# The second MLP's first layer as seven block products in place of eight

## Chip, core and metric

One core of a Trainium2 chip. The metric is the device time of one launch in microseconds, the median of the runs. TensorE (PE in the rows, PEld for its weight loads), VectorE (DVE), ScalarE (ACT) and GpSimd (POOL) each take their own instructions strictly in order; SyncE (SP) issues the DMAs, also in order.

## What is computed

Three stages, one behind the other, all in float32:

```python
attn = A @ Z @ C @ v                  # landmark attention, 4 batches of 576 tokens, 8 heads of 64
x = attn as [2304, 512]
h = x @ w_in                          # first MLP, 512 -> 2048 -> 512
x = (h - tanh(h)) @ w_out
h = x @ w_in2                         # second MLP, 512 -> 2048 -> 512
out = (h * tanh(softplus(h))) @ w_out2
```

The change is in the line `h = x @ w_in2`.

## The kernel before

Every matmul operand is split in a high part that TensorE takes exactly and a low part (`gg[:, 0]`, `gg[:, 1]` and the like); a product is three matmuls: high by high, high by low, low by high. ScalarE writes the high part by a copy, VectorE the low part by a subtraction.

**Stage one** runs in 128 slots (NS = 128; a batch has 32, each of 288 tokens by 128 hidden rows). A slot issues the first layer of its own block (`h1`), the second layer (`y1`) of the block three slots back (LAG = 3), and `vec`, the elementwise work. The attention of the next batch is strewn between. In the last 24 slots GpSimd is not used (`E()` gives VectorE). From slot 116 on the order of the engines is the order of the code; ahead of it a scheduler sets it. The results go to DRAM (`ys`).

**Stage two** has six chunks of 384 tokens by 16 blocks of 128 hidden rows: 96 slots. `h2` is 12 matmuls of 384 columns (4 pieces of the 512 inputs, 3 each), accumulated in one bank; ScalarE takes Mish of it twice (L600 writes the high part, L601 the whole), VectorE subtracts (L602); `o2`, three slots later, is 9 matmuls of 512 columns. The bank of `h2` is read by ScalarE alone, and the next slot but one writes it again.

Weights come as 64-bit numbers. `convert` brings them to float32 (a ScalarE cast at L133, a VectorE join at L137) and `split` to high and low (L102, L103). They are converted once, in the first two chunks of stage two, and all 32 blocks stay on the chip. Finished rows of the output leave from `raw` buffers, of which there are four, two tiles of 512 columns in each.

Of the kernel before, what the change touches and what calls it, by code (L numbers as in the profile page):

```python
# [29 lines left out]
def kernel(  # L30
# [150 lines left out]
    def convert(jobs, more=None):  # L181
        n = len(jobs)
        raws, st, parts2 = {}, {}, {}
        ahead = 4 if more else 3

        def fetch(i):
            if i < n:
                raws[i] = load_raw(jobs[i][0], more if more and i % 6 > 3 else None)
# [3 lines left out]
        for i in range(n + 2):  # L192
            if i < n:
                parts2[i] = f32_a(raws.pop(i), i)
            if i - 1 in parts2:
                where = jobs[i - 1][2]
                st[i - 1] = where() if where else st_p.tile([128, 512], F32, tag="y", name="y")
                yield from f32_b(*parts2.pop(i - 1), st[i - 1])
# [313 lines left out]
    W1o, W2i, W2o = {}, {}, {}  # L512
    yc, ops = {}, {}

    def tmp(s, tag, bufs=2):
        return tp[s >= NS].tile([128, width(s)], F32, tag=tag, name=tag, bufs=bufs)
# [15 lines left out]
    def cf(s):  # L532

        i = s - NS
        if i >= 32:
            return i // 16, i % 16
        n = PAIR - 16
        if i < 2 * n:
            return i % 2, i // 2
        return int(i >= PAIR), n + (i - 2 * n) % (16 - n)  # L540

    def h2(s):
        c, f = cf(s)
        y = yc[c]
        if s % 2 and s > NS + 32 + LAG:
# [391 lines left out]
```

## Time and profile before

| | |
|---|---|
| three runs | 840.97, 842.04 (median), 843.12 us |
| the profiled execution's own time | 840.79 us |
| its span | 839.0 us, granted clock 0.992 |
| TensorE busy | 811.1 us, 97% |
| VectorE, ScalarE, GpSimd busy | 473.0, 468.1, 179.4 us |

The span begins at the first and ends with the last record of the program; 1.8 us of the time lie around it. Times below are microseconds from the span's start. Stage two begins with the first `h2` at 428.7 us.

### The profile page before, as it was taken

The numbers are of one execution on the slowest core, as the hardware profiler recorded it, in microseconds if no ns is written. First come the engines' busy times: TensorE is split into PE (matmuls) and PEld (weight loads), VectorE is DVE, ScalarE is ACT, GpSimd is POOL, SyncE is SP. The second block draws the span as 40 slices with busy tenths as digits, with TensorE's granted clock in tenths as the row PEclk, the third lists the DMA queues.
The fourth block names the chain that finished last, engine by engine and source line by source line (L and its number), as shares of the span: only waits on it lengthen the run. The fifth ranks groups of instructions, "written<-read, shape, count | busy, mean of one in ns | idle before, by whom it ended". The sixth has DMA issues, their size and how long they took to land.

```text
span 839.0 us, 14649 instructions
## 1 busy us (share of the span) xinstructions
PE 811.1 (97%) x5528; PEld 696.4 (83%) x5528; DVE 473.0 (56%) x1093; ACT 468.1 (56%) x1163; POOL 179.4 (21%) x210
## 2 busy tenths in 40 slices
PE   4799999999999999999999999999999999999998
PEld 1446688789888988789999999999999999999996
DVE  7679999998799877899964744222112111111111
ACT  4576887888678976899765744233223223222221
POOL 0010006775588657840000000000000000000000
PEclk9699999999999999999999999999999999999999
DMA  9999341512135001451007741022002001000001
GB/s 323 321 336 356 111 138 52 170 67 90 54 104 182 2 30 38 136 165 47 3 1 270 253 132 45 1 66 76 0 1 69 8 1 57 9 1 24 15 1 38
DMA packets 34983, 79.57 MB, mean 95 GB/s; under 512 B 5472, under 2 KB 14176, under 8 KB 34912
## 3 DMA queue, kind: packets, MB, share of 16 engines
q1 hardware_dynamic: 33760, 74.45, 26.4%
q0 software_dynamic: 1152, 4.19, 1.2%
q8 instruction: 43, 0.70, 0.4%
q14 instruction: 28, 0.23, 0.1%
HBM read 65.00 MB, written 13.63 MB: 94 GB/s over the span
## 4 chain that ended last, share of the span: by engine, by line
PE 79%; DVE 9%; ACT 3%; POOL 2%; DMA 2%; issue 2%; DVEq 0%; SPq 0%; ACTq 0%; POOLq 0%
PE y L663 7%; PE y L659 7%; PE y L658 7%; PE h L553 5%; PE h L551 5%; PE h L552 5%; PE y L635 5%; PE y L639 5%; PE y L636 5%; PE h L525 4%; PE y L630 3%; PE m L217 3%; PE m L553 2%; PE m L551 2%; PE m L552 2%; DVE g L613 2%
## 5 line engine op out<-in xcount | busy, mean ns | idle before, releaser
L602 DVE TENSOR_TENSOR gg<-g,gg 128x384 fp32r<-128x384 f32 x96 | 53.6, 558 | 296.0 <-ACT g L601 296.0
L635 PE MATMUL y<-gg,w 128*128 128x288 f32 x448 | 133.7, 313 | 2.2 <-ACT raw L643 1.2
L636 PE MATMUL y<-gg,w 128*128 128x288 f32 x448 | 125.6, 295 | 0.0
L600 ACT ACTIVATE gg<-h 128x384 fp32r<-128x384 f32 x66 | 32.6, 494 | 142.3 <-PE h L553 142.3
L635 PEld LDWEIGHTS y<-gg,w 128*128 128x128 f32 x448 | 84.1, 188 | 22.2 <-issue 12.6
L659 PE MATMUL y<-w,gg 128*128 128x512 f32 x256 | 101.2, 395 | 0.0
L658 PE MATMUL y<-w,gg 128*128 128x512 f32 x256 | 100.8, 394 | 0.0
L639 PE MATMUL y<-gg,w 128*128 128x288 f32 x448 | 96.5, 297 | 0.4 <-POOL gg L103 0.2
L103 POOL TENSOR_TENSOR gg<-g,gg 128x288 fp32r<-128x288 f32 x80 | 69.5, 868 | 115.2 <-ACT gg L102 113.5
L663 PE MATMUL y<-w,gg 128*128 128x512 f32 x256 | 88.4, 396 | 0.0
L636 PEld LDWEIGHTS y<-gg,w 128*128 128x128 f32 x448 | 84.4, 188 | 1.1
L585 POOL TENSOR_SCALAR mk<-s 128x288 uint8<-128x288 f32 x80 | 77.4, 967 | 10.7 <-ACT s L579 4.4
L613 DVE COPY_PREDICATED g<-mk,th 128x288 f32<-128x288 uint8 x128 | 73.6, 575 | 4.2
L639 PEld LDWEIGHTS y<-gg,w 128*128 128x128 f32 x448 | 71.4, 188 | 1.9 <-POOL gg L103 1.7
L595 ACT ACTIVATE q<-q,bias_c 128x288 f32<-128x288 f32 x128 | 68.6, 536 | 2.3
L579 ACT ACTIVATE s<-h 128x288 f32<-128x288 f32 x128 | 52.0, 407 | 28.7 <-PE h L529 15.0
L591 DVE TENSOR_TENSOR g<-h,s 128x288 f32<-128x288 f32 x128 | 56.9, 445 | 18.4 <-ACT th L580 18.0
L553 PE MATMUL h<-yc,wj 128*128 128x384 f32 x192 | 64.6, 337 | 0.0
L600 ACT ACTIVATE gg<-m 128x384 fp32r<-128x384 f32 x30 | 14.8, 492 | 89.3 <-PE m L553 89.3
L552 PE MATMUL h<-yc,wj 128*128 128x384 f32 x192 | 64.4, 335 | 0.0
L551 PE MATMUL h<-yc,wj 128*128 128x384 f32 x192 | 64.4, 335 | 0.0
L609 DVE TENSOR_TENSOR g<-q,g 128x288 f32<-128x288 f32 x128 | 63.2, 494 | 1.4 <-ACT q L595 0.5
(162 smaller groups left out, 1833.4 us busy)
## 6 DMA issues: line engine op xcount, KB each, us to landing
w<-w1s SPq DMA_DIRECT2D x24, 512.0 KB, 4.7
raw<-in_w1i_dram SPq DMA_DIRECT2D x16, 511.8 KB, 6.4
raw<-in_w1o_dram SPq DMA_DIRECT2D x16, 511.8 KB, 6.8
raw<-in_w2i_dram SPq DMA_DIRECT2D x16, 511.8 KB, 4.7
raw<-in_w2o_dram SPq DMA_DIRECT2D x16, 511.8 KB, 4.2
ys<-raw SPq DMA_DIRECT2D x16, 288.0 KB, 2.3
out_dram<-raw SPq DMA_DIRECT2D x18, 256.0 KB, 2.3
v<-in_v_dram SPq DMA_DIRECT2D x8, 512.0 KB, 9.0
```

Of the source, the lines that this page charges most:

```text
L103: eng.tensor_tensor(out=L, in0=src, in1=f32(H), op=ALU.subtract)
L551: mm(p, w[:, 0, k, :], y[:, k, 0, :], start=(k == 0), stop=False)
L552: mm(p, w[:, 0, k, :], y[:, k, 1, :], start=False, stop=False)
L553: mm(p, w[:, 1, k, :], y[:, k, 0, :], start=False, stop=(k == 3))
L585: eng.tensor_scalar(out=mk, in0=e, scalar1=FT, scalar2=None, op0=ALU.is_ge)
L613: V.copy_predicated(out=g0, mask=mk0, data=t0)
L635: mm(yps[d], w[:, 0, c], gg[:, 0, :], start=(f == 0), stop=False)
L636: mm(yps[d], w[:, 1, c], gg[:, 0, :], start=False, stop=False)
L639: mm(yps[d], w[:, 0, c], gg[:, 1, :], start=False, stop=(f == NF - 1))
L658: mm(p, gg[:, 0, cs], w[:, 0, :], start=(f == 0), stop=False)
L659: mm(p, gg[:, 0, cs], w[:, 1, :], start=False, stop=False)
L663: mm(p, gg[:, 1, cs], w[:, 0, :], start=False, stop=(f == NF - 1))
```

## The change

Two chunks are one unit now (three units of 768 tokens), and two blocks of hidden rows one pair (eight). For a unit and a pair the product is a 2x2 by 2x2 product of blocks (inputs in two halves of 256, tokens in two of 384, hidden rows in two of 128). It is done with seven products of blocks in place of eight: four sums of blocks of x, four of the weights, seven of the results. So there are 24 **groups** (`group(k)`: unit k // 8, pair k % 8), each with seven **steps** p = 0 to 6. A step issues one product of 6 matmuls of 384 columns, then two units of the second layer of the group before (one in steps 5 and 6; 12 in all, 3 matmuls of 512 columns each), then `combine`.

- **Results.** `combine` adds a product from PSUM to a running sum in SBUF on VectorE (seven additions of 384, and one ScalarE copy at step 0). Mish reads the sums from SBUF, and the second Mish writes over its own input. The products have two banks (`ps_h`); the addition frees the bank for the next product but one.
- **Weights.** `w2_cycles` replaces `convert` for them. A cycle has seven parts, one per step; group k runs cycle k + 1 (cycle 0 lies in seven of the last 14 slots of stage one), and two last pieces of a group's own weights, the high and low part of `W2c[k][1]` slots 0 and 1, come in step 6 of the group before and step 0 of its own. Only the current weights of the first layer stay on the chip; `keep` writes them to DRAM (1.75 MB per pair), and groups 8 to 23 load them again (`w2c_load`, one group ahead).
- **Inputs.** `y_prep` makes the seven sums and parts of x for a unit: in nine slots from slot 102 on for the first unit (four sums of 768 columns on GpSimd), and next to groups 7 and 15 for the other two (two on GpSimd, two on VectorE). Its four loads go through the four `raw` buffers that the weights use.
- **Output.** The rows leave from the pool `st`, which has two buffers of 512 columns.

```diff
-    def h2(s):
-        ...
-        for k in range(4):
-            mm(p, w[:, 0, k, :], y[:, k, 0, :], start=(k == 0), stop=False)
-            mm(p, w[:, 0, k, :], y[:, k, 1, :], start=False, stop=False)
-            mm(p, w[:, 1, k, :], y[:, k, 0, :], start=False, stop=(k == 3))
-        hp[s] = p
+    WI = ((1, 2), (1, 1), (0, 1), (0, 3), (0, 2), (1, 0), (0, 0))
+    def product(k, p):
+        u, j = divmod(k, NJ)
+        t = ps_h.tile([128, 512], F32, tag="h", name="h")[:, 0:C2]
+        q, i = WI[p]
+        w, y = W2c[j][q], Y[u, p]
+        for a in range(2):
+            c = slice(128 * a, 128 * a + 128)
+            mm(t, w[:, i, 0, c], y[a][:, 0], start=(a == 0), stop=False)
+            mm(t, w[:, i, 0, c], y[a][:, 1], start=False, stop=False)
+            mm(t, w[:, i, 1, c], y[a][:, 0], start=False, stop=(a == 1))
+        hp[k, p] = t
+    def mish(k, blk, h):
+        ...
+        A.activation(out=gg[:, 0, :], in_=h, func=ACTF.Mish)
+        A.activation(out=h, in_=h, func=ACTF.Mish)
+        yield 0
+        V.tensor_tensor(out=gg[:, 1, :], in0=h, in1=f32(gg[:, 0, :]), op=ALU.subtract)
+        yield 0
+    def combine(k, p):
+        ...
+        elif p == 5:
+            to(xs[k, "u3"], xs[k, "u3"], ALU.subtract)
+            yield from mish(k, "21", xs[k, "u3"])
+        else:
+            to(xs[k, "u2"], xs[k, "u2"])
+            yield from mish(k, "12", xs[k, "u2"])
+        yield 1
+    def w2_cycles():
+        ...
+            cast("a", j)
+            if j:
+                lo(W2c[j - 1][1], 0, rows[j - 1][:, 0:2])
+                keep(j - 1)
+                yield 0
+            o_join("c", j - 1)
+            yield 0
+            cast("d", j - 1)
+            yield 1
+        ...
+            fetch("d", j)
+            if i:
+                W = W2c[j] = [P_p.tile([128, 4, 2, 256], F32R, tag="P", name="P") for q in range(2)]
+                hi(W[1], 2, X[:, 0:1])
+                hi(W[0], 0, X[:, 2:6])
+                minus(X[:, 1], X[:, 2], X[:, 4])
+            yield 1
+            fetch("b", j + 1)
+            if i:
+                lo(W[1], 2, X[:, 0:1])
+                yield 0
+                minus(X[:, 0], X[:, 1], X[:, 3])
+            yield 1
+            cast("c", j)
+            if i:
+                hi(W[1], 0, X[:, 0:2])
+                lo(W[0], 0, X[:, 2:6])
+            yield 1
+    def y_prep(u):
+        ...
+        a21, a22, a11, a12 = load(0, 1), load(1, 1), load(0, 0), load(1, 0)
+        ...
+        tt(G, s1, a21, a22, ALU.add)
+        yield 1
+        tt(V, s2, s1, a11)
+        yield from halves(0, a11)
+        ...
+    def o_evict(u, tt, on_vector):
+        o = st_p.tile([128, 512], F32, tag="y", name="y")
+        if on_vector:
+            V.tensor_copy(out=o, in_=ops[u, tt])
+        else:
+            A.activation(out=o, in_=ops[u, tt], func=ACTF.Copy)
+        r0 = (2 * u * NTT + tt) * 128
+        nc.sync.dma_start(out=out[r0:r0 + 128, :], in_=o)
+    UNITS = (2, 2, 2, 2, 2, 1, 1)
+    def group(k, bg2):
+        if k:
+            units = o2_units(k - 1)
+        for p in range(7):
+            product(k, p)
+            if k:
+                for _ in range(UNITS[p]):
+                    next(units)
+                gens = []
+            else:
+                cur[0] = NS + p // 2
+                if p < 2 * LAG:
+                    y1(NS - LAG + p // 2, p % 2)
+                gens = [vec(cur[0])] if p % 2 == 0 and p < 4 else []
+        ...
+            mix = bg2(k, p)
+            for g in mix:
+                part(g)
+            parts(gens + [combine(k, p)] + mix)
```

Where stage one meets stage two, on VectorE. Before, three results of stage one (`gg`, `g`) stand between the first two Mish subtractions:

```order
L103 TENSOR_TENSOR gg_6280<-g_6207,gg_6280 128x288 [waits Activation_49]
L609 TENSOR_TENSOR g_6243<-q_6244,g_6243 128x288 [waits DVE_49]
L602 TENSOR_TENSOR gg_6285<-g_6284,gg_6285 128x384 [waits Activation_49]
L613 COPY_PREDICATED g_6243<-mk_6245,th_6242 128x288 [waits DVE_49]
L103 TENSOR_TENSOR gg_6316<-g_6243,gg_6316 128x288 [waits Activation_49]
```

Now (L100 is the old L103, L682 the old L609, L182 writes a low part of the weights `P`, L158 joins weights, L806 adds a product `h` to a sum, L671 and L672 are the first elementwise steps of the last slot):

```order
L182 TENSOR_TENSOR P_6106<-X_5843,P_6106 128x4x256
L665 TENSOR_SCALAR mk_6253<-s_6249 128x288 [waits Activation_49]
L686 COPY_PREDICATED g_6215<-mk_6217,th_6214 128x288 [waits DVE_49]
L671 TENSOR_TENSOR g_6251<-h_6227,s_6249 128x288 [waits Activation_49]
L672 TENSOR_TENSOR th_6250<-h_6227,th_6250 128x288
L100 TENSOR_TENSOR gg_6279<-g_6215,gg_6279 128x288 [waits Activation_49]
L682 TENSOR_TENSOR g_6251<-q_6252,g_6251 128x288 [waits DVE_49]
L182 TENSOR_TENSOR P_6107<-X_5843,P_6107 128x2x256
L686 COPY_PREDICATED g_6251<-mk_6253,th_6250 128x288 [waits DVE_49]
L158 SCALAR_TENSOR_TENSOR y_6291<-raw_5918,top0_127 128x512 [waits DMAHW4_49]
L806 TENSOR_TENSOR u2_6307<-x_6284,h_6294 128x384 [waits PE_49,Activation_49]
```

The low part `P_6107` (slots 0 and 1 of the first group's weights), which the product of step 1 reads, has moved in behind the stage-one work, and the first addition behind that and a join.

Steps 5, 6 and the next step 0 of a group, on ScalarE. Before, in the slots with conversion, a Mish pair alternates with casts and high parts, and waits for TensorE alone:

```order
L600 ACTIVATE gg_6677<-h_6654 128x384 [waits PE_49]
L601 ACTIVATE g_6676<-h_6654 128x384
L133 ACTIVATE top1_112<-raw_6598 128x512 [waits DMAHW5_49,DVE_49,Activation_49]
L102 ACTIVATE wj_6686<-y_6647 128x512
L133 ACTIVATE top0_111<-raw_6606 128x512 [waits DMAHW6_49,DVE_49,Activation_49]
L102 ACTIVATE w_6694<-y_6682 128x512
```

Now (L796 and L797 the Mish pair, L130 the cast, L178 the high part of weights, L809 the copy of step 0):

```order
L796 ACTIVATE gg_6569<-x_6525 128x384 [waits DVE_49]
L797 ACTIVATE x_6525<-x_6525 128x384 [waits Activation_49]
L796 ACTIVATE gg_6588<-u2_6477 128x384 [waits DVE_49]
L797 ACTIVATE u2_6477<-u2_6477 128x384 [waits Activation_49]
L130 ACTIVATE top0_127<-raw_6505 128x512 [waits DMAHW2_49]
L178 ACTIVATE P_6553<-X_6479 128x2x256
L809 ACTIVATE x_6608<-h_6595 128x384 [waits PE_49]
```

The same steps on VectorE now (L799 is the subtraction behind Mish, L185 a sum of weights):

```order
L806 TENSOR_TENSOR x_6525<-x_6525,h_6558 128x384 [waits DVE_49,PE_49]
L182 TENSOR_TENSOR P_6553<-X_6479,P_6553 128x256 [waits DMAHW1_49,Activation_49]
L799 TENSOR_TENSOR gg_6569<-x_6525,gg_6569 128x384 [waits Activation_49]
L185 TENSOR_TENSOR X_6479<-X_6479 128x256 [waits DVE_49]
L806 TENSOR_TENSOR u2_6477<-u2_6477,h_6577 128x384 [waits PE_49]
L182 TENSOR_TENSOR P_6552<-X_6479,P_6552 128x4x256 [waits DMAHW0_49]
L799 TENSOR_TENSOR gg_6588<-u2_6477,gg_6588 128x384 [waits Activation_49]
L182 TENSOR_TENSOR P_6553<-X_6479,P_6553 128x2x256 [waits DVE_49,Activation_49]
```

Mish waits for VectorE, the second of a pair for the first, and the last row, which the next group's step 1 needs, stands behind both pairs.

The last rows on ScalarE. Before:

```order
L600 ACTIVATE gg_9228<-m_9205 128x384 [waits PE_49]
L601 ACTIVATE g_9227<-m_9205 128x384 [waits DVE_49]
L672 ACTIVATE raw_9255<-y_8891 128x512 [waits DMAHW0_49,PE_49]
L672 ACTIVATE raw_9264<-y_8899 128x512 [waits DMAHW1_49,PE_49]
L932 UNCONDITIONAL_BRANCH
```

Now (one more row, y_9546, is a copy on VectorE between the last two):

```order
L853 ACTIVATE y_9522<-y_8708 128x512 [waits DMAHW2_49,PE_49]
L853 ACTIVATE y_9528<-m_8725 128x512 [waits DMAHW3_49,PE_49]
L853 ACTIVATE y_9534<-m_8729 128x512 [waits DMAHW0_49,PE_49,Activation_49]
L853 ACTIVATE y_9540<-y_8687 128x512 [waits DMAHW1_49,PE_49,Activation_49]
L853 ACTIVATE y_9552<-y_8704 128x512 [waits DMAHW3_49,PE_49,Activation_49]
```

Six tiles leave at the end in place of three, and from the third on each waits for the DMA of the tile two before it.

## Rows read from the trace of the kernel before

**Rows 1.** The page's line of engines: busy us, share of span, instructions.

```profile
PE 811.1 (97%) x5528; PEld 696.4 (83%) x5528; DVE 473.0 (56%) x1093; ACT 468.1 (56%) x1163; POOL 179.4 (21%) x210
```

**Rows 2.** Windows: stretch, length, busy by engine (count), granted clock, DMA share, GB/s.

```profile
30.00:40.00 10.00, 7.15 (x61) 2.67 (x58) 4.68 (x10) 5.58 (x11) 0.00 (x0) 0.50 0.93 312
...
390.00:400.00 10.00, 9.22 (x70) 8.99 (x69) 10.00 (x26) 9.26 (x26) 0.00 (x0) 1.00 0.17 61
...
600.00:650.00 50.00, 50.00 (x253) 45.15 (x252) 8.19 (x15) 13.28 (x30) 0.00 (x0) 1.00 0.10 29
```

**Rows 3.** Timeline of TensorE, one slot of stage two: start, length, what.

```profile
703.04 0.33 PE L551 MATMUL h<-yc,wi 128*128 128x384 f32 x1
...
705.13 0.39 PE L658 MATMUL y<-w,gg 128*128 128x512 f32 x1
...
707.22 0.33 PE L551 MATMUL m<-yc,wi 128*128 128x384 f32 x1
```

**Rows 4.** VectorE by form over the span: busy, mean ns, idle before.

```profile
L591 DVE TENSOR_TENSOR g<-h,s 128x288 f32<-128x288 f32 x128 | 56.9, 445 | 18.4 <-ACT th L580 18.0
L602 DVE TENSOR_TENSOR gg<-g,gg 128x384 fp32r<-128x384 f32 x96 | 53.6, 558 | 296.0 <-ACT g L601 296.0
...
L137 DVE SCALAR_TENSOR_TENSOR y<-raw,top 128x512 uint32<-128x512 uint32 x32 | 21.9, 685 | 0.2
...
L103 DVE TENSOR_TENSOR w<-y,w 128x512 fp32r<-128x512 f32 x16 | 11.1, 691 | 1.6 <-ACT w L102 1.6
```

**Rows 5.** Timeline of VectorE at two places in stage one.

```profile
361.08 1.06 DVE L609 TENSOR_TENSOR g<-q,g 128x288 f32<-128x288 f32 x1
...
372.96 0.44 DVE L609 TENSOR_TENSOR g<-q,g 128x288 f32<-128x288 f32 x1
373.33 0.44 DVE L103 TENSOR_TENSOR gg<-g,gg 128x288 fp32r<-128x288 f32 x1
```

**Rows 6.** Timeline, from a product's end to VectorE, in stage two.

```profile
709.13 0.33 PE L553 MATMUL m<-yc,wi 128*128 128x384 f32 x1
...
709.50 0.49 ACT L600 ACTIVATE gg<-m 128x384 fp32r<-128x384 f32 x1 [0.27 <-PE m L553]
...
709.88 0.49 ACT L601 ACTIVATE g<-m 128x384 f32<-128x384 f32 x1
...
710.40 0.56 DVE L602 TENSOR_TENSOR gg<-g,gg 128x384 fp32r<-128x384 f32 x1 [0.52 <-ACT g L601]
```

**Rows 7.** Timeline of ScalarE where stage one ends.

```profile
425.69 0.44 ACT L582 ACTIVATE q<-s 128x288 f32<-128x288 f32 x1
426.17 0.54 ACT L595 ACTIVATE q<-q,bias_c 128x288 f32<-128x288 f32 x1
...
429.33 1.28 ACT L570 ACT_TABLE_LOAD   x1
```

**Rows 8.** Timeline of ScalarE in stage two: a cast, then a high part.

```profile
451.15 0.80 ACT L133 ACTIVATE top<-raw 128x512 f16<-128x512 bf16 x1
451.80 0.61 ACT L102 ACTIVATE w<-y 128x512 fp32r<-128x512 f32 x1
```

**Rows 9.** ScalarE by form over the span.

```profile
L102 ACT ACTIVATE w<-y 128x512 fp32r<-128x512 f32 x16 | 9.9, 619 | 0.0
```

**Rows 10.** The chain that ended last, merged: start, length, what (two matmuls of 288 columns).

```profile
431.46 0.27 PE y L639 x2
```

**Rows 11.** DMA issues by kind: KB each, median us to landing.

```profile
out_dram<-raw SPq DMA_DIRECT2D x18, 256.0 KB, 2.3
...
yf<-ys SPq DMA_DIRECT2D x16, 144.0 KB, 2.7
```

**Rows 12.** Timeline of GpSimd; the second row is its last instruction.

```profile
360.70 1.13 POOL L103 TENSOR_TENSOR gg<-g,gg 128x288 fp32r<-128x288 f32 x1
...
368.60 0.93 POOL L585 TENSOR_SCALAR mk<-s 128x288 uint8<-128x288 f32 x1
```

**Rows 13.** Timeline of the end.

```profile
834.91 0.60 ACT L672 ACTIVATE raw<-y 128x512 f32<-128x512 f32 x1 [0.33 <-PE y L663]
```

More of the change, by code (lines that the diff above doesn't have):

```diff
@@ L148, in whole_job, with w2c_load @@
+    def w2c_load(j):
+        W = W2c[j] = [P_p.tile([128, 4, 2, 256], F32R, tag="P", name="P") for q in range(2)]
+        for q in range(2):
+            n = 4 - q
+            nc.sync.dma_start(out=f32(W[q][:, 0:n].rearrange("p n t c -> p n (t c)")), in_=w2s[j][q][:, 0:n, :])
     def whole_job(src, dst, i):
@@ L193, in convert @@
             if i < n:
[L194 to L198, printed above, removed]
+                halves[i] = f32_a(raws.pop(i), i)
+            if i - 1 in halves:
+                st[i - 1] = jobs[i - 1][2]()
+                yield from f32_b(*halves.pop(i - 1), st[i - 1])
             fetch(i + ahead)
@@ new lines, in vec, with mask_op @@
+            e = tmp("s")
+            t = tmp("th")
+            g = tmp("g", 4)
+            q = tmp("q")
+            mk = t1_p.tile([128, HS], U8, tag="mk", name="mk")
+            A.activation(out=e, in_=h, func=ACTF.Square)
+            A.activation(out=t, in_=h, func=ACTF.Tanh)
+            with tc.high_priority(40):
+                A.activation(out=q, in_=e, func=ACTF.Exp, scale=FK)
+            def mask_op(eng):
+                eng.tensor_scalar(out=mk, in0=e, scalar1=FT, scalar2=None, op0=ALU.is_ge)
@@ new lines, in o2_units @@
+    def o2_units(k):
+        u, j = divmod(k, NJ)
+        for i, blk in enumerate(("11", "22", "21", "12")):
+            f = 2 * j + (blk[1] == "2")
+            for t in range(NTT):
+                tt = t + NTT * (blk[0] == "2")
+                first, last = j == 0 and i < 2, j == NJ - 1 and i >= 2
+                if first:
+                    pool, tag = (ps_y, "y") if tt < 4 else (ps_m, "m")
+                    ops[u, tt] = pool.tile([128, 512], F32, tag=tag, name=tag)
+                q, gg, w = ops[u, tt], gs[k, blk], W2o[f]
+                cs = slice(128 * t, 128 * t + 128)
+                mm(q, gg[:, 0, cs], w[:, 0, :], start=first, stop=False)
+                mm(q, gg[:, 0, cs], w[:, 1, :], start=False, stop=False)
+                mm(q, gg[:, 1, cs], w[:, 0, :], start=False, stop=last)
+                if last:
+                    o_evict(u, tt, k == NU * NJ - 1 and tt == NTT - 2)
+                yield
@@ L707, in pipeline @@
         with tc.manual_schedule():
-            for s in range(SWITCH, NT_S + LAG):
+            for s in range(SWITCH, NS):
                 slot(s, bg)
+            for k in range(NU * NJ):
+                group(k, bg2)
+            k = NU * NJ - 1
+            for _ in o2_units(k):
+                pass
     def vec_only(g, rate=[1]):
@@ L896 @@
+        pipeline(bg, bg2)
 _OUTS = [((2304, 512), "float32")]
```

340 lines of the change are left out of this document (186 added, 154 removed).

## Prediction

> **What bounds the kernel now.** I read the page's engines first: TensorE is busy 97% of the span [rows 1]. A busy TensorE need not be one that never waits, so next the windows: in stage two it is busy 50.00 of 50 us at the full granted clock, with VectorE at 8.2 and ScalarE at 13.3 [rows 2]. The timeline of one slot gives the price of a matmul: from the first of 384 columns at 703.04 to the first of 512 at 705.13 lie 12 matmuls, and 9 more to 707.22 [rows 3], so 0.174 us for 384 columns and 0.232 us for 512. A slot is 4.18 us, and 96 of them fill stage two. So TensorE alone sets the end of stage two, and whatever shortens its list counts in full until another engine is late. Stage one's last slots are different: VectorE is busy 10.00 of 10 us at 390 us and TensorE 9.22 [rows 2]; there VectorE is the bound.
>
> **What the change removes.** 24 groups have 42 matmuls of 384 columns each where 48 stood: 144 x 0.174 = 25.1 us. Form, weight loads and columns of the rest stay. The Trainium skill, "TensorE: Matmul & The Clock Gate", section Back-to-back issue gap, gives columns / 2.4 + 2.5 ns, which would be 162.5 ns, 23.4 us for the 144, and a total 1.7 us higher than mine; the slot above disagrees with it, and I use the row.
>
> **What it adds.** The products' results are no longer only read by Mish. Per group VectorE gets 7 additions and 4 low parts of 384, and in the first unit a cycle of weights. By the forms [rows 4] a VectorE element costs 1.04 ns (0.691 for 512 less 0.558 for 384), so 0.545 for a 384 addition that reads PSUM (0.445 for 288), 0.425 for 256, 1.22 for 1024. A group: 7 x 0.545 + 4 x 0.558 + 4 joins x 0.685 + 2 x 0.691 (second layer) + sums 0.691 + 2 x 0.425 + low parts 0.425 + 0.691 + 1.22 = 14.0 us. The group's matmuls are 42 x 0.174 + 36 x 0.232 = 15.7 us. It fits, and back to back an operation starts 0.07 us before the one ahead ends (372.96 and 373.33 [rows 5]), but the margin is thin, VectorE takes things in order, and between an addition and its low part it waits for two Mish. So I walk the chains, group time 0 being the start of the group's first product; steps 0 to 4 last 2.44 us, steps 5 and 6 1.74.
>
> **Groups 2 to 7, one wait each.** A product can be read 0.2 us after the next could start (709.13 plus 0.17, read at 709.50 [rows 6]). Step 5's product ends at 13.24, so VectorE adds at 13.44: 0.55. Then Mish, and the second Mish, which waits for the first: a wait on the own engine costs 0.04 (425.69 + 0.44, next at 426.17 [rows 7]); 0.04 + 0.53 + 0.49 + 0.04. Low part 0.48, weights' sum 0.35, step 6's addition 0.55 (all behind each other on VectorE), Mish 0.04 + 0.53 + 0.38, cast 0.65 (451.15 to 451.80 [rows 8]), high part of the weights 0.62 [rows 9], low part 0.04 + 0.69 + 0.04. Together 6.0, so 19.46; TensorE wants this low part for the third matmul of the next step 1, at 15.68 + 2.44 + 0.35 = 18.47. **1.0 us per group, six groups: 6.0.** Bounds: 0 if the two Mish overlap as at L600 and L601 and the cast comes earlier, 1.7 if nothing of it overlaps; 0 to 10.
>
> **The seam: group 0 and the next step 1.** The last stage-one slot leaves ScalarE with a Mish table to load (1.28 [rows 7]) and now with a cast and a high part ahead of it; on VectorE the low part `P_6107` stands behind four rows of the last slot and behind the 1024 low part. I walk it: ScalarE about 1 us late at the start, cast to 1.9, high part to 2.54, stage-one high part to 2.8, and VectorE's wait for that puts `P_6107` at 4.3, where TensorE wants it at 2.2: 2.1 us. Queued behind this row on VectorE are the last pick of stage one, a join and the first addition, and each frees something: TensorE's bank, the cast's buffer, the last `y1`. A step is 1.83 us here (6 x 0.174 + 6 x 0.13 of stage one [rows 10]) against some 2.3 of VectorE's work, so the additions stay late and TensorE waits for a bank at products 5 and 6 (0.5 and 0.4) and at group 1's first (0.65). Then the chain of the last paragraph runs once more, from an addition at 15.05, with the output copies of stage one on ScalarE ahead of its first Mish (free at 16.4), and ends at 21.9, where without any wait group 1's step 1 would want it at 14.8. **7.1** in all, bounds 3 and 10.
>
> **Inputs of units two and three, next to groups 7 and 15.** They bring VectorE 14 low parts and two sums of 768 (0.96): 9.7 us beside 5.8 of the results, and in group 7 the last weights. There, too, a load of x waits for a `raw` buffer that a join of step 0 frees (at 4.1), lands 2.7 later [rows 11], and the sum that needs it holds VectorE to 7.0, with step 2's addition (6.9) behind it. From then on VectorE is two us late and the banks run out: 0.35 + 1.7 + 1.1 + 1.0 at the products up to group 8's second, and 0.4 by the Mish waits. Group 15 has its loads early: 1.4. **6.0**, bounds 2 and 10. GpSimd's sums lie beside this: VectorE's L609 took 1.06 us while GpSimd worked (from 360.70 for 1.13) and 0.44 later [rows 5, 12], so a 768 sum, 2.5 us by the mask's 0.93 for 288, may hold VectorE for up to that; this is in the upper bound. The Trainium skill, "SBUF — State Buffer", section SBUF: two separate sides, states it as a lock on a port that both share, held for a whole instruction, for VectorE operations with two SBUF inputs; the two rows agree, and by it the two sums of group 7 would cost 5 us more if neither falls in a gap.
>
> **Stage one.** VectorE's extra work of the last 24 slots was 8 low parts, 6 joins, 6 splits (12.6 us); now 14 low parts, 2 joins and the first sums (12.3). I take 0. The GpSimd sums stand ahead of its last mask (at 368.60 [rows 12]) and may push it by 5 us, which VectorE, the bound there, waits out: 0 to +4.
>
> **End.** After the last matmul one copy (0.60 at 834.91 [rows 13]) and one DMA (2.3 [rows 11]) remain. Now six tiles leave through two buffers, a buffer's round is 0.60 + 2.3 + 0.1 = 3.0, and a tile comes every 0.70. The fifth and sixth tile start at +2.5 and +3.2 after the last matmul in place of 0: **+3.2**, bounds 2 and 4. Groups 8 and 16 have the same queue, hidden by 2.4 us until a bank is missed.
>
> Hidden: the DMAs of `keep` and of the weights (1.75 + 2 MB per 16 us, 235 GB/s; [rows 2] show 312), and the reloads, one group ahead.
>
> **Sum.** -25.1 + 6.0 + 7.1 + 6.0 + 0 + 3.2 = -2.8 against the profiled execution's own 840.79: 838.0; the median of the runs is 1.25 higher, so **839.2**. 0.3% of it (2.5 us) is about what a measurement tells from no change.
>
> **Rivals.**
> - *Waits hidden.* If ScalarE and VectorE run the chains with their overlaps at every hop, the six waits vanish, the seam costs 3, the inputs 2, the end 2 to 3.2: 842.0 - 25.1 + 8 = 825. For it: VectorE has 1.7 us of 15.7 left by the sum, and 1.9 more by the overlap (27 operations by 0.07); against: the order puts a chain of ten operations across two engines, and a chain gains nothing from idle time elsewhere.
> - *VectorE becomes the bound in the first unit* (ends slower). If its four waits for a Mish pair per group (about 1.0 us each) are not filled, a group is 14.0 + 4 = 18.0 us, 2.3 over the matmuls, for eight groups 18.7 in place of the 7.0 that I charge to seven of them (six, and one in the seam): 851. It decides from a group of 17.0 us on. Against it: between addition and low part nearly every step has a weight operation that waits for neither.
> - *TensorE's clock falls at the seam.* The granted clock was 0.50, the lower level, at 30 to 40 us with TensorE busy 7.15 of them [rows 2]. In the seam it is busy about 8 in 10. Ten us at that level would cost 5: 844, and the same would come in groups 7 and 8.
> - *The removal does not tell,* because weight loads set the pace: then 384 and 512 columns would cost the same; [rows 3] refute it, and loads go in the same number.
>
> **Chances.** The sum's case, 834 to 846: 0.55 (0.23 faster, 0.25 no change, 0.07 slower). Hidden: 0.24, faster. VectorE bound: 0.13, slower. Clock: 0.06, half no change. The last: 0.02, no change. So faster 0.47, same 0.30, slower 0.23. The range of 8 in 10 runs from the better half of the hidden case to the VectorE case: 826 to 850.
>
> **What would show it.** Right: 1008 product matmuls at 0.174; about 1 us without TensorE at step 1 of groups 2 to 7, released by VectorE's low part; 6 to 8 us of waits in the first 24 us of stage two; 4 to 6 in groups 7 and 8; none in groups 9 to 14; a last DMA some 6 us after the last matmul. Wrong: waits at every step of the first unit, or none at all.

## The result: 847.04 us, 5 us slower

The changed kernel takes 847.04 us (five runs, 846.66 to 850.32) where the kernel before takes 842.04 (840.97 to 843.5 beside it): ratio 1.007, interval 1.0045 to 1.0095. That lies inside the range of 826 to 850, on the other side of no change than forecast. The profiled execution has a span of 844.9 us, 5.9 more than the 839.0 of before.

The removal did what it was costed at. What came back was as large: waits, and slow stretches behind them, ate the gain of stage two to within 0.1 us, and stage one and the end each became some 3 us longer.

### The profile page after: what moved, and what is told of

Same layout as the page of the kernel before. It is cut to its first block, busy times and chain, and to the rows that moved or that the text cites. A ratio compares the mean times of both kernels' runs of the same rounds, so it can differ in the third digit from the quotient of the medians.

```text
span 844.9 us, 14775 instructions
## 1 busy us (share of the span) xinstructions
PE 797.4 (94%) x5384; PEld 673.9 (80%) x5384; DVE 595.0 (70%) x1315; ACT 510.1 (60%) x1213; POOL 196.9 (23%) x218
## 5 line engine op out<-in xcount | busy, mean ns | idle before, releaser
L796 ACT ACTIVATE gg<-x 128x384 fp32r<-128x384 f32 x72 | 37.8, 525 | 171.4 <-DVE x L806 170.9
L783 PE MATMUL h<-yk,P 128*128 128x384 f32 x288 | 99.0, 344 | 13.2 <-ACT P L178 5.9
L708 PEld LDWEIGHTS y<-gg,w 128*128 128x128 f32 x448 | 84.4, 188 | 21.9 <-issue 12.6
L785 PE MATMUL h<-yk,P 128*128 128x384 f32 x288 | 98.1, 341 | 1.4 <-DVE P L182 0.7
L784 PE MATMUL h<-yk,P 128*128 128x384 f32 x288 | 97.1, 337 | 0.0
L100 POOL TENSOR_TENSOR gg<-g,gg 128x288 fp32r<-128x288 f32 x80 | 70.1, 876 | 112.9 <-ACT gg L99 110.6
L799 DVE TENSOR_TENSOR gg<-x,gg 128x384 fp32r<-128x384 f32 x72 | 40.2, 558 | 61.2 <-ACT x L797 61.2
L806 DVE TENSOR_TENSOR x<-x,h 128x384 f32<-128x384 f32 x72 | 39.8, 553 | 60.7 <-PE h L785 60.4
L686 DVE COPY_PREDICATED g<-mk,th 128x288 f32<-128x288 uint8 x128 | 75.6, 591 | 4.6
L843 PE MATMUL y<-w,gg 128*128 128x512 f32 x192 | 76.3, 398 | 0.0
L842 PE MATMUL y<-w,gg 128*128 128x512 f32 x192 | 76.3, 397 | 0.0
L841 PE MATMUL y<-w,gg 128*128 128x512 f32 x192 | 75.7, 394 | 0.0
L783 PEld LDWEIGHTS h<-yk,P 128*128 128x128 f32 x288 | 54.5, 189 | 25.4 <-ACT P L178 8.9
L742 POOL TENSOR_TENSOR yf<-raw 128x768 f32<-128x768 f32 x3 | 6.3, 2104 | 283.3 <-ACT x L797 168.2
L671 DVE TENSOR_TENSOR g<-h,s 128x288 f32<-128x288 f32 x128 | 56.8, 444 | 18.9 <-ACT th L660 18.4
```

The costliest lines, as they stand in the source:

```text
L100: eng.tensor_tensor(out=L, in0=src, in1=f32(H), op=ALU.subtract)
L686: V.copy_predicated(out=g0, mask=mk0, data=t0)
L708: mm(yps[d], w[:, 0, c], gg[:, 0, :], start=(f == 0), stop=False)
L783: mm(t, w[:, i, 0, c], y[a][:, 0], start=(a == 0), stop=False)
L784: mm(t, w[:, i, 0, c], y[a][:, 1], start=False, stop=False)
L785: mm(t, w[:, i, 1, c], y[a][:, 0], start=False, stop=(a == 1))
```

## Profile after

The page's line of engines, beside [rows 1]: TensorE is busy 13.7 us less, VectorE 122 us more.

```profile
PE 797.4 (94%) x5384; PEld 673.9 (80%) x5384; DVE 595.0 (70%) x1315; ACT 510.1 (60%) x1213; POOL 196.9 (23%) x218
```

The waits of TensorE in stage two, as the waits' view sums them: total, times, longest, all in us. There was not one before.

```profile
PE h L783 <- ACT P L178: 5.9, 7, 2.6
PE h L783 <- DVE u L806: 3.8, 4, 1.3
PE h L783 <- DVE x L806: 2.2, 2, 1.4
PE h L783 <- issue: 1.4, 2, 1.1
PE h L783 <- DVE th L672: 1.2, 1, 1.2
PE h L785 <- DVE P L182: 0.7, 1, 0.7
```

L783 to L785 are a product's matmuls. Seven times one waits for the high part of the weights (L178); of these six are groups 2 to 7, one (2.6) is group 1. These 15.2 us are the idle time alone; behind a wait the first two matmuls start about 0.28 apart in place of 0.174, and some run at the lower clock. So a loss is counted from starts: the distance of two starts less 0.174, or less 0.232 behind 512 columns and 0.13 behind 288.

The windows, to be read beside [rows 2] (stretch, length, busy by engine, granted clock, DMA share, GB/s):

```profile
435.00:440.00 5.00, 4.10 (x17) 3.81 (x18) 4.16 (x9) 4.45 (x7) 0.00 (x0) 0.76 0.99 369
455.00:460.00 5.00, 5.00 (x18) 4.26 (x18) 2.65 (x5) 2.09 (x4) 0.00 (x0) 0.69 1.00 337
470.00:520.00 50.00, 48.05 (x233) 41.39 (x232) 38.18 (x70) 30.27 (x54) 0.00 (x0) 1.00 0.64 237
570.00:575.00 5.00, 2.91 (x14) 1.95 (x12) 3.90 (x8) 1.88 (x4) 0.00 (x0) 1.00 0.99 338
600.00:650.00 50.00, 50.00 (x251) 44.98 (x251) 18.91 (x35) 13.74 (x27) 0.00 (x0) 1.00 0.32 112
```

At two places behind the seam the granted clock falls to the lower level for part of the window; where most of the groups' waits lie VectorE is busy 38.18 of 50 us; next to groups 7 and 8 TensorE is busy 2.91 of 5 us at the full clock; groups 9 to 14 have no wait.

**Where each part of the launch ends.** Of every kernel four times were read from its timeline: ScalarE's first operation of slot 96 of stage one (`Square` of h), the first product of stage two, the start of the last matmul, and the span. The columns on the right are their differences.

| kernel | time | slot 96 | first product | last matmul | span | slot 96 to stage two | stage two | end |
|---|---|---|---|---|---|---|---|---|
| before | 842.04 | 343.45 | 428.66 | 834.49 | 839.0 | 85.2 | 405.8 | 4.5 |
| changed | 847.04 | 343.82 | 432.01 | 837.71 | 844.9 | 88.2 | 405.7 | 7.2 |
| e1 end buffers | 844.37 | 344.18 | 432.35 | 838.39 | 842.6 | 88.2 | 406.0 | 4.2 |
| e2 high part first | 845.22 | 345.45 | 433.60 | 836.16 | 843.4 | 88.2 | 402.6 | 7.2 |
| e3 cycles ahead | 838.51 | 343.66 | 434.61 | 829.56 | 836.8 | 91.0 | 395.0 | 7.2 |
| e4 inputs later | 848.26 | 345.19 | 432.86 | 839.19 | 846.4 | 87.7 | 406.3 | 7.2 |
| e5 sums on VectorE | 841.38 | 346.48 | 436.81 | 832.06 | 839.3 | 90.3 | 395.3 | 7.2 |
| e6 inputs earlier | 835.85 | 346.30 | 437.20 | 826.87 | 834.1 | 90.9 | 389.7 | 7.2 |
| e7 before, 42 products | 818.29 | 345.89 | 431.12 | 811.99 | 816.5 | 85.2 | 380.9 | 4.5 |
| e8 all repairs | 824.09 | 343.67 | 433.98 | 817.27 | 821.5 | 90.3 | 383.3 | 4.2 |
| e9 GpSimd longer | 825.26 | 344.33 | 435.75 | 818.81 | 823.0 | 91.4 | 383.1 | 4.2 |
| e10 sums fourfold | 829.44 | 344.23 | 436.75 | 823.47 | 827.7 | 92.5 | 386.7 | 4.2 |

Up to slot 96 the kernels do the same work, and yet this stretch differs by up to 3.0 us from run to run. What makes that stays open; the three columns on the right are free of it, and single times are not. The times of e1, e2, e4 to e7 and e10 are of one execution each, the others medians of four or five; so the experiments are read from the columns. One thing moves between two of these: in e3, e5, e6 and e8 to e10 TensorE is idle for 1.15 to 1.17 us right ahead of the first product, and the changed kernel, e1, e2 and e4 have such a wait right behind it (1.17 at 435.25), so some 1.3 us by starts count to stage one in the former and to stage two in the latter. Changed against before: +0.4 to slot 96, +3.0 to stage two, -0.1 in stage two, +2.7 at the end.

## The experiments

All but e7 start from the changed kernel; e5 and e6 contain e3's edit, e9 and e10 all of e8.

**e7, the removal alone.** The kernel before, with 6 of the first layer's 48 matmuls left out in every four slots (a quarter of the inner sum of half the blocks is missing).

```diff
-        for k in range(4):
+        n = 4 - s % 2
+        for k in range(n):
             mm(p, w[:, 0, k, :], y[:, k, 0, :], start=(k == 0), stop=False)
...
-            mm(p, w[:, 1, k, :], y[:, k, 0, :], start=False, stop=(k == 3))
+            mm(p, w[:, 1, k, :], y[:, k, 0, :], start=False, stop=(k == n - 1))
```

> The kernel before, of whose first layer's matmuls every second slot of stage two leaves out the last three of twelve, a quarter of its sum for half of the blocks: 144 matmuls of 384 columns fewer, no sums, no new chains. It prices the removal alone. Theory (each removed matmul is worth 0.174 us, since TensorE alone sets stage two): 25.1 us less, 817. Rival (a slot's length is set by something else as well, a bank or ScalarE's two Mish): less than 20 us.

Measured: stage two 380.87 us where before has 405.83, 24.96 less. So the term of -25.1 was right, and the rival that the removal does not tell is out. By the formula that the Trainium skill ("TensorE: Matmul & The Clock Gate", section Back-to-back issue gap) gives for an isolated matmul it would have been 23.4, an estimate; the measurement sides with the spacing of [rows 3].

**e1, the end.**

```diff
-        o = st_p.tile([128, 512], F32, tag="y", name="y")
+        if u < NU - 1:
+            o = st_p.tile([128, 512], F32, tag="y", name="y")
+        else:
+            n = (tt + NTT) % (2 * NTT)
+            if n % 2 == 0:
+                ops["o"] = raw_f32()
+            o = ops["o"][:, 512 * (n % 2):512 * (n % 2) + 512]
```

> Only the eviction of the last unit's six output tiles is changed: they leave through halves of the four raw buffers, as before the change, in place of two small buffers. Theory (a queue of tiles through two buffers): in the changed kernel the last matmul starts at 837.71 and the span ends at 844.9, 7.2 us later, where the kernel before has 4.5; the fifth and sixth copy wait 8.6 and 2.2 us for a transfer to leave. With free buffers 7.2 falls to about 4.5, the span by 2.7, nothing else moves. Rival (the last transfer's own time sets the end, whatever buffer it leaves): less than 0.5 us.

In the changed kernel the timeline of the end has the last matmul's start, then the two last copies, both waiting for a transfer that left their buffer:

```profile
837.71 0.39 PE L843 MATMUL y<-w,gg 128*128 128x512 f32 x1
...
840.47 0.69 DVE L851 COPY y<-y 128x512 f32<-128x512 f32 x1 [8.64 <-DMA out_dram<-y]
840.96 0.60 ACT L853 ACTIVATE y<-y 128x512 f32<-128x512 f32 x1 [2.19 <-DMA out_dram<-y]
```

Measured: 7.2 falls to 4.2 us, and no other column moves by more than 0.3. The queue through two buffers was the cause.

**e2, the chain of groups 2 to 7.**

```diff
-            cast("c", j)
             if i:
                 hi(W[1], 0, X[:, 0:2])
+            cast("c", j)
+            if i:
                 lo(W[0], 0, X[:, 2:6])
```

> Only ScalarE's order in the last step of a cycle is changed: the high part of the weights that the next group's step 1 needs goes ahead of a cast that nothing needs yet (0.78 us, 0.64 from start to start). Theory (one chain of operations over two engines is late, VectorE has room): the wait at step 1 of groups 2 to 7, 1.19 us each in the changed kernel with a group's period at 16.84, falls to about 0.5, the period to 16.2; six times, 4 us less in all. Rival (VectorE's work sets the group's period): the period stays at 16.8 and the same idle time turns up at another step. Second rival (the pair of Mish is what is late, not the place of the cast): less than 0.2 per group.

The changed kernel's timeline of one such wait, on three engines (start, length, what, idle before):

```profile
483.23 0.56 DVE L806 TENSOR_TENSOR x<-x,h 128x384 f32<-128x384 f32 x1 [0.16 <-PE h L785]
...
487.32 0.78 ACT L130 ACTIVATE top<-raw 128x512 f16<-128x512 bf16 x1
...
487.96 0.61 ACT L178 ACTIVATE P<-X 128x512 fp32r<-128x512 f32 x1
488.60 0.69 DVE L182 TENSOR_TENSOR P<-X,P 128x512 fp32r<-128x512 f32 x1 [0.59 <-ACT P L178]
488.62 0.44 PE L783 MATMUL h<-yk,P 128*128 128x384 f32 x1 [0.54 <-ACT P L178]
489.35 0.45 PE L785 MATMUL h<-yk,P 128*128 128x384 f32 x1
```

Step 1 would start at 487.93. Its first matmul waits for the high part (to 488.57), its third for the low part (to 489.29); the cast at 487.32 stands ahead of both. With the high part first, TensorE's timeline there reads:

```profile
488.41 0.39 PE L844 MATMUL y<-w,gg 128*128 128x512 f32 x1
...
488.71 0.45 PE L784 MATMUL h<-yk,P 128*128 128x384 f32 x1
488.99 0.34 PE L785 MATMUL h<-yk,P 128*128 128x384 f32 x1
489.43 0.44 PE L786 MATMUL h<-yk,P 128*128 128x384 f32 x1
```

The first matmul hardly waits (it starts 0.30 behind one of 512 columns, where 0.23 is the least), the third still loses 0.27. Measured: the period, from one group's `x<-h` copy on ScalarE to the next, falls from 16.84 to 16.20, 0.64 for the 0.64 by which the high part moved; stage two is 3.1 us shorter. Less than 4, since group 7 did not gain (its step 1 still loses 0.81 at 554.26). VectorE's work is the same, so it is not what sets the period.

**e3, cycles ahead.**

```diff
-        early = [NS - x for x in (14, 12, 10, 7, 5, 3, 1)]
+        early = [NS - x for x in (14, 12, 11, 10, 8, 6, 4, 2)]
```

> The cycles of weight work run one step ahead: eight steps in stage one, in slots 14, 12, 11, 10, 8, 6, 4 and 2 before its end, in place of seven in slots 14, 12, 10, 7, 5, 3 and 1; so the low part that step 1 of a group needs is made in step 6 of the group before, and the first one before stage two starts. The work is the same. Theory (chains are late, engines have room): the waits at step 1 of groups 2 to 7 (7.2 us in all) vanish and the period falls to 15.7; of the 9.0 us at the seam the parts that wait for weights' parts (0.8 at 436.5 and 2.8 with the half clock after it at 453.4) go, some 5 us; the inputs of unit two get their buffers one step earlier, 1 to 3 us less in groups 7 and 8; stage one may end up to 1.5 us later, as a step more lies there. In all 11 to 14 us less, 833 to 836. Rival (VectorE's work sets the period of a group in unit one): the period stays at 16.8, and the time within 3 us of the changed kernel's 847.

Measured: 838.51, ratio to before 0.9957 (0.994 to 0.9974): one list of numbers turns the change from 0.7% slower to 0.4% faster. The period of groups 2 to 6 is 15.66 with no wait, and from the first product to group 2's start no clock falls. The column of stage one grows by 2.8 us, but 1.3 of these are the wait that now stands ahead of the first product; the other 1.5 are what I gave for an eighth step there, where VectorE is the bound. The forecast of 833 to 836 missed for another reason, a new wait in group 7:

```profile
551.85 0.40 PE L843 MATMUL m<-w,gg 128*128 128x512 f32 x1
557.85 0.69 PE L783 MATMUL h<-yk,P 128*128 128x384 f32 x1 [5.60 <-DVE x L806]
558.33 0.52 PE L784 MATMUL h<-yk,P 128*128 128x384 f32 x1
558.65 0.52 PE L785 MATMUL h<-yk,P 128*128 128x384 f32 x1
```

With the waits ahead of it gone, TensorE comes to step 1 of group 7 3.2 us earlier (552.08 for 555.26). The inputs' loads land in time for a first sum at 551.99 and no sooner; VectorE waits for it from 547.8 to 553.8, and an addition that frees the bank stands behind, at 557.25. The prediction had the other transfers hidden; here, from 544 to 554, the DMA engines are busy throughout (share 0.96 to 1.09 in stretches of 2 us), and these loads take 3.8 to 6.2 us to land where the walk had 2.7. Whether the late issue or the other traffic sets that is not separated. Behind so long a wait the matmuls run at the lower of the two clock levels (0.32 apart, length 0.52) until 562: 2.2 us more.

**e4, inputs later in stage one.**

```diff
-        yearly = [NS - 26] + [NS - 24 + i + i // 3 for i in range(8)]
+        yearly = [NS - 24] + [NS - 22 + i + i // 3 for i in range(8)]
...
-            if s == yearly[0] - 1:
+            if s == NS - 27:
```

> Only the sums and parts of the first unit's inputs are moved, two slots later in stage one (from 26 to 24 slots before its end), behind the last masks and low parts of GpSimd; the work and its engines are the same. Against the kernel before, the changed one is 0.4 us late at slot 104, 2.6 at slot 105, 6.2 at slot 112 and 3.4 where stage two starts. Theory A (GpSimd's three sums of 2.1 us stand ahead of its last masks and low parts, for which TensorE waits): slot 105 is back to 0.4, and stage two starts about 2.5 us earlier. Theory B (VectorE, the bound of these slots, has 14 low parts in ten slots): the lag arises two slots later and stage two starts within 1 us of where it does.

Measured: slot 105 is as late as ever (2.2 us against slot 96, as in the changed kernel), stage two 0.5 earlier. It does not separate the theories: the order ahead of slot 116 is the scheduler's, and it left the sums where they were. They start at 367.48, 1.37 later than the 366.11 of the changed kernel, and this run was 1.37 later at slot 96 already. Only some low parts moved (slot 112 is 3.5 late against slot 96, for 5.9).

**e5, sums on VectorE.**

```diff
-            (G if u == 0 else eng).tensor_tensor(out=o, in0=x, in1=y, op=op)
+            V.tensor_tensor(out=o, in0=x, in1=y, op=op)
```

> The cycles stand one step ahead as in the run before it, and the sums of the inputs that GpSimd made (three of the first unit in stage one, two of each later unit) are made on VectorE. Theory (GpSimd's sums hold VectorE): in stage one VectorE's rows beside these sums took 1.97, 0.98 and 2.21 us where the same operations take 0.48, 0.54 and 0.54 elsewhere, 3.6 us in all; three sums on VectorE cost 0.97 each, 2.9. So the lag against the kernel before at slot 105, which was 2.4, falls to 1 or less, and stage two starts 0.5 to 1.5 us earlier, in spite of more work on VectorE; in group 7 the wait of 5.8 us falls to 3.5 to 4.5, since the first sum takes 0.97 in place of 1.8 and two low parts no longer take 2.6. Rival (VectorE's amount of work is what counts in stage one): stage two starts 2 to 3 us later.

The changed kernel's timeline of GpSimd, VectorE and TensorE from 366 us on shows what is meant:

```profile
366.11 1.95 POOL L742 TENSOR_TENSOR yf<-raw 128x768 f32<-128x768 f32 x1
366.44 1.97 DVE L686 COPY_PREDICATED g<-mk,th 128x288 f32<-128x288 uint8 x1
...
368.31 1.26 DVE L614 TENSOR_TENSOR P<-m,P 128x512 fp32r<-128x512 f32 x2
...
371.10 1.83 POOL L742 TENSOR_TENSOR raw<-raw 128x768 f32<-128x768 f32 x1
371.14 2.21 DVE L752 TENSOR_TENSOR yk<-raw,yk 128x384 fp32r<-128x384 f32 x1
371.19 0.54 PE L712 MATMUL y<-gg,w 128*128 128x288 f32 x2 [1.94 <-POOL gg L100]
```

L686 and L752 read two operands from SBUF, and each ends 0.35 to 0.42 after the GpSimd sum beside it (0.48 and 0.54 elsewhere). L614 reads one from PSUM and takes its usual 0.63 beside the next sum. Measured with the sums on VectorE: slot 105 is 0.1 us late against slot 96 (e3: 2.2), and stage two comes 0.6 earlier than in e3, though VectorE makes four sums (not three, as I had counted; 4.2 us) more. The wait in group 7 is 3.85 in place of 5.77. So the sums cost VectorE no less where GpSimd made them, and the rival's 2 to 3 us later did not come. The edit takes away two things at once, though: the hold, and a low part that GpSimd made behind two of its sums, for which TensorE waited 1.94 us (at 371.19), most of slot 105's 2.2. What tells them apart is that VectorE is idle for 0.2 us in all from 364 to 404 us in the changed kernel: a late TensorE cost it nothing there. These windows, from slot 96 to the first product, have the rest (before, then changed):

```profile
343.45:428.66 85.21, 82.21 (x619) 76.38 (x618) 81.22 (x211) 74.69 (x195) 20.51 (x22) 1.00 0.25 81
```

```profile
343.82:432.01 88.19, 83.26 (x618) 76.44 (x617) 84.19 (x208) 72.07 (x192) 28.42 (x26) 1.00 0.24 78
```

VectorE, the third number after the length, is idle 4.0 us in both; the 3.0 by which the stretch grew are its busy time.

**e6, inputs of later units earlier.** The loads go out at step 3 of group 6 in place of step 6, two of them into buffers of their own.

```diff
+            if u and th == 0:
+                t = p2["yl"].tile([128, 2, C2], F32, tag="yl", name="yl")
+            else:
+                t = raw_f32()[:, 0:2 * C2].rearrange("p (a n) -> p a n", a=2)
...
         tt(V, s2, s1, a11)
+        if u:
+            yield 1
...
-            if j == NJ - 2 and p == 6 and u + 1 < NU:
+            if j == NJ - 2 and p == 3 and u + 1 < NU:
                 gens["y"] = vec_only(y_prep(u + 1))
+            if j == NJ - 2 and p in (3, 6) and u + 1 < NU:
                 mix.append(gens["y"])
```

> The cycles stand one step ahead, and the inputs of units two and three are loaded three steps earlier, two of the four into buffers of their own, with one step between the sums and the first parts; the sums' engines and all work are the same. Theory (a late transfer holds VectorE, which takes its list in order): the wait of 5.8 us in group 7 falls to under 1, and the stretch at half clock behind it (some 4 us) goes with it: 8 to 10 us less than 838.5, 829 to 831. The two waits of 1.2 and 1.1 us at the start of group 8 and those in groups 15 and 16 (2.3) stay, since they come from parts that stand between additions. Rival (VectorE has too much to do in group 7, or GpSimd's sums hold it): at least 3 of the 5.8 us stay.

Measured: stage two 389.7, 5.3 less than in e3. The wait of 5.77 and the 2.2 at the lower clock are gone; the gain is below 8 to 10 because I had put the clock at 4, and because 1.1, 0.4 and 0.8 stand there now (at 546.06, 551.6 and 561.58), of which the first is GpSimd's sum again:

```profile
542.79 1.91 POOL L745 TENSOR_TENSOR raw<-yl,raw 128x768 f32<-128x768 f32 x1
542.92 2.20 DVE L804 TENSOR_TENSOR gg<-x,gg 128x384 fp32r<-128x384 f32 x1
...
545.37 0.54 DVE L811 TENSOR_TENSOR x<-x,h 128x384 f32<-128x384 f32 x1
...
546.06 0.41 PE L788 MATMUL h<-yk,P 128*128 128x384 f32 x1 [0.97 <-DVE x L811]
```

**e8, all repairs.** e1, e3, e5, e6, and for later units the low parts one step behind their high parts:

```diff
...
+            for p in range(8):
+                if p:
+                    yield from low(p - 1, T[p - 1])
+                if p == 2:
+                    tt(V, a21, a11, a21)
+                if p == 3:
+                    tt(V, s2, a12, s2)
+                if p < 7:
+                    high(p, T[p])
+                yield 1
...
```

> All repairs together: cycles one step ahead, all sums on VectorE, inputs of later units loaded earlier into own buffers, their low parts one step behind their high parts so that an addition never stands behind a wait for ScalarE, and the last tiles through the raw buffers. By the sum of the theories' terms: 838.5, less 3.0 for the end (measured alone), less 8 to 10 for the inputs of unit two, less 2 to 3 for the waits at the start of group 8 and in groups 15 and 16, less 0 to 1.5 in stage one: 821 to 826, faster than the kernel before by 16 to 21 us. If the repairs overlap or VectorE becomes the bound of group 7 with the sums added: 828 to 833.

Measured: 824.09, ratio to before 0.9796 (0.9774 to 0.9817). A window of the first unit:

```profile
470.00:520.00 50.00, 50.00 (x250) 44.86 (x249) 40.88 (x75) 32.43 (x58) 0.00 (x0) 1.00 0.69 260
```

Stage two is 383.3 us; the 405.8 of before less the 25.0 of e7 would be 380.9. So 2.4 are left there; the 5.1 us in stage one, with the 1.3 ahead of the first product, are not repaired.

**e9, GpSimd longer in stage one.**

```diff
-        return G if 24 <= cur[0] < NS - 24 else V
+        return G if 24 <= cur[0] < NS - 16 else V
```

> All repairs, and GpSimd makes the masks and low parts of stage one for eight slots more, up to 16 slots before its end in place of 24. In the run with all repairs VectorE is busy 10.00 of 10 us from 370 to 400 us, and stage two starts 5.3 us later than in the kernel before. Theory A (VectorE's amount of work sets these slots): a mask (0.21 from start to start) and a low part (0.37) less in each of eight slots give up to 4.6 us back, 820 to 822. Theory B (GpSimd's work holds VectorE's rows that have both inputs beside it): what is taken from VectorE comes back as longer rows of picks, products and input parts, and the time stays within 1.5 us of 824 or grows.

Measured: 825.26, ratio to before 0.9798 (0.9772 to 0.9824), the same as e8; stage two comes 1.1 later. VectorE by form from 372 to 395 us (busy, mean ns, idle), first of e8, then of e9:

```profile
L755 DVE TENSOR_TENSOR yk<-raw,yk 128x384 fp32r<-128x384 f32 x7 | 3.8, 549 | 0.0
L682 DVE TENSOR_TENSOR g<-q,g 128x288 f32<-128x288 f32 x8 | 3.6, 449 | 0.0
...
L672 DVE TENSOR_TENSOR th<-h,th 128x288 f32<-128x288 f32 x8 | 3.6, 448 | 0.0
```

```profile
L682 DVE TENSOR_TENSOR g<-q,g 128x288 f32<-128x288 f32 x9 | 5.6, 627 | 0.0
L755 DVE TENSOR_TENSOR yk<-raw,yk 128x384 fp32r<-128x384 f32 x6 | 5.0, 826 | 0.0
...
L672 DVE TENSOR_TENSOR th<-h,th 128x288 f32<-128x288 f32 x9 | 4.0, 442 | 0.0
```

Theory B: by its own bound of 1.5 us. The forms that read both operands from SBUF grow from 449 to 627 and from 549 to 826 ns beside GpSimd; L672, which reads h from PSUM, does not.

**e10, VectorE's room.**

```diff
-                minus(X[:, 4:6, :], X[:, 1:3, :], X[:, 0:2, :])
+                for _ in range(4):
+                    minus(X[:, 4:6, :], X[:, 1:3, :], X[:, 0:2, :])
```

> All repairs, and in each cycle one sum of the weights' blocks (128 x 512, 0.61 us from start to start) is made four times in place of once: 1.8 us more of VectorE's work per group of the first unit, 15 us in all, with the same result. In the run with all repairs VectorE is busy 40.88 of 50 us there, 12.8 of a group's 15.66. Theory (VectorE has room, chains alone made the waits): within 2 us of 824; the period of groups 2 to 6 stays 15.66. Rival of the prediction (VectorE bounds the first unit, with its waits for pairs of Mish at 18.0 us a group): the period grows by up to 1.8 us a group, 10 to 13 us in all.

Measured: 829.44. By stage against e8: 2.2 us in stage one, where VectorE is the bound and the 1.8 us added there are paid in full; 1.5 more at one step of group 0; and the period 15.80 in place of 15.66, 0.14 of the 1.8 added. Neither forecast fits the whole, but for groups 2 to 6 the rival falls: VectorE has room there, at 45.93 busy of 50 us beside a TensorE without a wait (to be read beside e8's window):

```profile
470.00:520.00 50.00, 50.00 (x248) 44.08 (x246) 45.93 (x82) 32.52 (x59) 0.00 (x0) 1.00 0.69 258
```

## Why the prediction was wrong

By its own sum, each term beside what was measured (losses from starts, as above):

| term | predicted | measured |
|---|---|---|
| removal | -25.1 | -25.0 (e7) |
| groups 2 to 7 | 6.0 | 7.2 |
| the seam | 7.1 | 9.0 |
| inputs of units two and three | 6.0 | 9.4 (6.8 and 2.6) |
| rest of stage two, where nothing waits | 0 | -0.7 (against e7) |
| stage one | 0 | 3.0 |
| end | 3.2 | 2.7 |
| sum | -2.8 | +5.6, and 0.4 ahead of slot 96 make 6.0 of the span's 5.9 |

The waits stood where they were walked to, save those for a bank at the seam; nearly all were sized low, and together with stage one and the end they were larger than the gain. Each of the five terms that came back lies within its own bounds. Step by step:

- **Groups 2 to 7: right, 0.2 each short.** The walk gave 6.02 us from step 5's addition to the end of the low part; the rows of e2's section give 483.23 to 489.29, 6.06. The third matmul starts 1.07 late (489.35, wanted at 488.28) where 1.0 was forecast, 0.7 of it already at the first matmul, which waits for the high part, and the next is 0.12 late again. This tail was not in the sum. e2 and e3 show the cause by making the wait shorter and then zero.
- **The seam: right to 0.2 us, without the clock.** The changed kernel's timeline:

```profile
435.25 0.42 PE L783 MATMUL h<-yk,P 128*128 128x384 f32 x1 [1.17 <-DVE th L672]
...
435.75 0.68 DVE L182 TENSOR_TENSOR P<-X,P 128x512 fp32r<-128x512 f32 x1
...
436.49 0.44 PE L785 MATMUL h<-yk,P 128*128 128x384 f32 x1 [0.65 <-DVE P L182]
...
453.38 0.69 DVE L182 TENSOR_TENSOR P<-X,P 128x512 fp32r<-128x512 f32 x1 [0.58 <-ACT P L178]
453.40 0.44 PE L783 MATMUL h<-yk,P 128*128 128x384 f32 x1 [2.64 <-ACT P L178]
...
455.10 0.63 PE L841 MATMUL y<-w,gg 128*128 128x512 f32 x1
455.52 0.63 PE L842 MATMUL y<-w,gg 128*128 128x512 f32 x1
```

  From the first product at 432.01 the two low parts end at 4.4 and 22.1; the walk had 4.3 and 21.9, so 7.3 for its 7.1. That TensorE waits for a bank at products 5 and 6 and at group 1's first did not happen: it had been slowed in another way, at the lower clock, from 437.9 to 441. This first fall should have cost nothing of its own (argued, not tested), since the second low part was the same hurdle for a TensorE that came earlier. The second, behind the wait of 2.64, has matmuls of 512 columns 0.43 apart until 458 and cost 1.6: the clock rival's mechanism on top of the likeliest case, at less than a third of its price. e3, with no long wait there, has no fall.
- **Stage one: the step that failed.** "I take 0", it said, as VectorE's own work hardly changes, with 0 to +4 for GpSimd's sums, through a last mask that comes late. The mask did come 4.4 late (373.02 for 368.60), but VectorE had no idle time before it. What cost was the hold of VectorE's own rows: 1.5, 0.4 and 1.7 longer beside the first three sums, 0.9 beside the fourth. Of these 4.5 us 3.0 came out as delay, and the windows in e5's section show it as VectorE's busy time; the other 1.5 are, by difference, work that it no longer has ahead of stage two. That the hold comes with the sums is shown by e5, which moves them, and that such work costs no less on GpSimd than on VectorE by e9.
- **Inputs: the same step.** The hold was put into the upper bound and not into the sum. In group 7 (POOL is GpSimd; the low parts are two rows):

```profile
560.77 0.96 DVE L742 TENSOR_TENSOR yf<-yf,raw 128x768 f32<-128x768 f32 x1 [1.84 <-DMA raw<-ys]
560.80 2.63 POOL L742 TENSOR_TENSOR raw<-raw 128x768 f32<-128x768 f32 x1 [8.69 <-DMA raw<-ys]
561.64 2.68 DVE L752 TENSOR_TENSOR yk<-raw,yk 128x384 fp32r<-128x384 f32 x2
...
566.87 0.56 DVE L752 TENSOR_TENSOR yk<-yf,yk 128x384 fp32r<-128x384 f32 x1 [1.48 <-ACT yk L751]
```

  Two low parts take 2.68 where two elsewhere take 1.02 (569.35): 1.7. The rest is the chain that the walk had only for two steps: high part behind a pair of Mish, low part behind it, addition behind that, 1.1 to 1.6 us of idle VectorE at every step to 580. e8, with the low parts a step later (and the sums on VectorE, and earlier loads), loses 0.5 there in place of 6.8; the step alone was not run.
- **End: right**, 2.7 for 3.2 (e1).
- **The rivals.** VectorE as the bound: refuted for the groups by e2, e3 and e10; right for stage one alone, of which the prediction itself had said it. Waits hidden, 825: what a better order gives, 824.09 in e8, but not the order that was written. That the two numbers agree is in part luck: 825 has 3 at the seam and 2 at the inputs, where e8 has 2.4 left in all of stage two, and nothing in stage one, where e8 has 5.1.

That the range held is in part luck: its upper end came from VectorE as the bound of the groups, at 851, which the runs refute. The direction failed first of all because one mechanism, seen in [rows 5, 12], stood in the sum at zero at two places: stage one's 3.0 and the 1.7 in group 7 are more than half of the 8.4 by which the sum was short. With them in it the sum would have been +1.9, some 844: on the right side, if still within what the prediction called no change. The rest is 1.9 at the seam, 1.7 more at the inputs and 1.2 in groups 2 to 7, less 0.5 at the end and 0.7 where nothing waits.

## What to carry to other kernels

A saving on the bound engine can be lost where work now crosses engines, so walk every other engine's list to the microsecond there; here 25 us of removed matmuls were lost to 25 us of waits and slow stretches in stage two, though VectorE was busy only 38 of 50 us where most of the groups' waits lie. Order is the cheap remedy: the same cycle of work one step earlier was worth more than 8 us, and 11.7 more of stage two came from keeping operations that wait for another engine or a transfer from standing ahead of the addition that frees a bank, with the sums on VectorE (e3 to e8). Where the rows show one engine holding another that is the bound, put the hold into the sum and not only into its upper bound; here four GpSimd sums of 8.5 us held VectorE for 4.5.

## What the runs showed of the hardware

- A GpSimd operation on SBUF holds a VectorE operation with two SBUF operands until about its end: 0.48 becomes 1.97 beside a sum of 1.95, 0.54 becomes 2.21 beside one of 1.83; and GpSimd's own sums of 768 vary from 1.83 to 2.81. A VectorE operation with one operand in PSUM keeps its time (448 and 442 ns). The Trainium skill, "SBUF — State Buffer", section SBUF: two separate sides, states this as a lock on a port pair that the two engines share, held for a whole instruction; the trace agrees in each of these rows.
- The lower clock came behind single waits of 2.64 and 5.60 us, and behind 1.17 and 0.65 close together, and lasted 3 to 4 us of full work; with five waits of 0.89 to 1.35, starting 3 to 4 us apart (564 to 579), it did not come. Nor is a wait of one length always followed by the same: in stage one the changed kernel kept the full clock behind a wait of 1.94 (371.19; 1.00 over 373 to 378), and e1, with the same instructions and a wait of 1.93 there, did not (0.66).
- TensorE does not resume at its pace: behind a wait the first spacing of two matmuls was 0.25 to 0.29 in place of 0.174 (435.25, 453.40, 488.62, 564.84).
